# Splitting the first channel product of an MLP-mixer kernel into 49 block products on two levels instead of seven on one

**Chip and metric.** One core of one Trainium2 chip. The metric is the device time of one launch in microseconds (us); lower is better.

## What is computed

Attention without softmax, a root-mean-square norm, then an MLP mixer: first over tokens, then over channels. All in fp32.

```python
kv  = einsum('bhsd,bhse->bhde', k, v)            # B=8, H=8, S=576, D=64
out = einsum('bhsd,bhde->bhse', q, kv)
x   = out / sqrt(mean(out*out, -1) + 1e-6) * g_norm      # -> (B, S, 512)
u   = x + (relu(x.T @ w_tok1) @ w_tok2).T                # token mixing, 576 -> 256 -> 576
y   = u + relu(u @ w_ch1) @ w_ch2                        # channel mixing, 512 -> 1536 -> 512
```

The channel mixing is nine groups of 512 tokens, each one 512x512x1536 product (the "first" product), a relu, and one 512x1536x512 product (the "second").

## The kernel before

Both channel products are done with seven block products in place of eight (Strassen's scheme, in Winograd's form): the operands are cut in 2x2 blocks, sums of the blocks are formed (`mix_ch1`, `mix_ch2` for the weights once, `mix_u` for the tokens in each group), seven block products run on TensorE, and their results are combined. VectorE adds PSUM (where the kernel's matmuls put their sums) to what ScalarE copied out to SBUF (where its other tiles lie). Besides the four blocks of the relu the second product needs sums of them, `s1` to `s4`.

```python
def channel1(g, d):                         # three times a group, each for 512 of the 1536 columns
    ...
    def product(n, ps, start, stop):
        for w in range(W):                  # W = 2
            for c in range(2):
                nc.tensor.matmul(ps[:, w], lhsT=w_ch1[:, n - 1, c, ts(W * d + w, P)],
                                 rhs=uc[g][n - 1][:, c], ...)        # 256 tokens
    product(1, p1, True, False);  nc.scalar.copy(t1, p1)
    product(6, p6, True, True);   add(u2, p6, t1)
    product(7, p7, True, False);  add(u3, p7, u2)
    product(5, p5, True, False);  add(a22, p5, u3);  nc.scalar.activation(a22, a22, AF.Relu)
    product(2, p1, False, True);  nc.scalar.activation(a11, p1, AF.Relu)
    product(4, p7, False, True);  add(a12, p7, u2);  nc.scalar.activation(a12, a12, AF.Relu)
    product(3, p5, False, True);  add(s3, p5, u2)
    # max-and-add: relu of s3 and the sum in one instruction of VectorE, 512 columns
    nc.vector.scalar_tensor_tensor(out=s1, in0=s3, scalar=0.0, in1=a22, op0=max, op1=add)
    nc.vector.scalar_tensor_tensor(out=s3, in0=s3, scalar=0.0, in1=a11, op0=max, op1=subtract)
    nc.gpsimd.tensor_tensor(out=s2, in0=s1, in1=a11, op=subtract)
    nc.gpsimd.tensor_tensor(out=s4, in0=a12, in1=s2, op=subtract)
# (cut: channel2, with the same seven steps; attention; token mixing; decoding of the weights)
```

Of the kernel before, what the change touches and what calls it, by code (L numbers as in the profile page):

```python
# [9 lines left out]
F32 = mybir.dt.float32  # L10
U32 = mybir.dt.uint32
AF = mybir.ActivationFunctionType
# [5 lines left out]
def kernel(  # L18
# [29 lines left out]

    nc = tc.nc
    P = 128  # L50
# [11 lines left out]
    FH = DCH // 2  # L62
    NS = NF // 2
# [11 lines left out]
    stage = pool("stage", 2, "right")  # L75
    right = ExitStack()
    xp = pool("xp", 9, "right", right)
    hp_ = pool("hp", 2, "right", right)
    left = ExitStack()
# [9 lines left out]
    w_tok1 = consts.tile([P, JJ, DTOK], F32, name="w_tok1")  # L89
    w_tok2 = consts.tile([P, NTOK, S], F32, name="w_tok2")  # L90

    w_ch1 = consts.tile([P, 7, 2, FH], F32, name="w_ch1")
    w_ch2 = consts.tile([P, 7, NS, DH], F32, name="w_ch2")
# [5 lines left out]
    def do(f, *a):  # L99
        return lambda: f(*a)  # L100

# [72 lines left out]



    A1 = {(0, 0): 0, (0, 1): 1, (1, 1): 3, (1, 0): 6}
    B2 = {(0, 0): 0, (1, 0): 1, (1, 1): 2, (0, 1): 6}

    FQ = FH // 2  # L180

    def get_ch1(i, c, h):
        return block(FQ, lambda raw: [(raw, words(moe_w_ch1)[ts(c, P), ts(2 * i + h, FQ)])],
                     w_ch1[:, A1[i, c // 2], c % 2, ts(h, FQ)])

    def get_ch2(f):
        a, b = B2[f // NS, 0], B2[f // NS, 1]
        return block(DM, lambda raw: [(raw, words(moe_w_ch2)[ts(f, P)])],
                     w_ch2[:, a:b + 1:b - a, f % NS],
                     lambda raw: raw.rearrange("p (h n) w -> p h n w", h=2))  # L190

    def combine(o, a, b, op):
        nc.vector.tensor_tensor(out=o, in0=a, in1=b, op=op)  # L193

    def mix_ch1(c):
        w = [w_ch1[:, i, c] for i in range(7)]
        combine(w[4], w[6], w[3], ALU.add)
        combine(w[5], w[4], w[0], ALU.subtract)
        combine(w[6], w[0], w[6], ALU.subtract)
        combine(w[2], w[1], w[5], ALU.subtract)  # L200

    def mix_ch2(i):

        w = [w_ch2[:, n, 2 * i:2 * i + 2] for n in range(7)]
        combine(w[4], w[6], w[0], ALU.subtract)
        combine(w[5], w[2], w[4], ALU.subtract)
        combine(w[6], w[6], w[2], ALU.subtract)
        combine(w[3], w[1], w[5], ALU.subtract)
# [8 lines left out]
    def attention(pair):  # L217
# [13 lines left out]
        def norm(o_ps, c, n):  # L231
            o = o_ps.rearrange("p t (h d) -> p (t h) d", d=D)
            x = X[pair, c] = xp.tile([P, n, DM], F32, name="x", tag=f"x{n}", bufs=9 if n == 2 else 2)
            x3 = x.rearrange("p t (h d) -> p (t h) d", d=D)
            shape = [P, n * H, 1]
            nc.scalar.activation(x3, o, AF.Square)
            ms = work.tile(shape, F32, name="ms")
            nc.vector.tensor_reduce(ms, x3, axis=AX.X, op=ALU.add)  # L238
            nc.vector.tensor_scalar(out=ms, in0=ms, scalar1=1.0 / D, scalar2=EPS,
                                    op0=ALU.mult, op1=ALU.add)  # L240

            root = work.tile(shape, F32, name="root")
            nc.scalar.activation(root, ms, AF.Sqrt)
            inv = work.tile(shape, F32, name="inv")
            nc.vector.reciprocal(inv, root)
            nc.vector.scalar_tensor_tensor(out=ms, in0=ms, scalar=0.5, in1=inv,
                                           op0=ALU.mult, op1=ALU.mult)
            nc.vector.scalar_tensor_tensor(out=root, in0=root, scalar=0.5, in1=ms,
                                           op0=ALU.mult, op1=ALU.add)
            nc.vector.reciprocal(inv, root)  # L250
            nc.vector.tensor_mul(x3, o, inv.to_broadcast([P, n * H, D]))  # L251
            nc.gpsimd.tensor_mul(x3, x3, g_sb.to_broadcast([P, n * H, D]))  # L252
# [77 lines left out]
    def turn_u(g, i, psum):  # L330
        if i == 0:
            uT[g] = late["u"].tile([P, NC, J * P], F32, name="uT")
        pt = psum()
        for c in range(NC):
            nc.tensor.transpose(pt[:, c], xg[g][:, i, ts(c, P)], ident)  # L335
        nc.scalar.copy(uT[g][:, :, ts(i, P)], pt)  # L336

    def mix_u(g):
        b = {(i, j): uT[g][:, 2 * i:2 * i + 2, ts(j, 2 * P)] for i in range(2) for j in range(2)}
        t1, t2, t4 = (late["u"].tile([P, 2, 2 * P], F32, name=f"t{i}") for i in (1, 2, 4))  # L340
        sub = lambda o, x, y: nc.vector.tensor_tensor(out=o, in0=x, in1=y, op=ALU.subtract)
        sub(t1, b[0, 1], b[0, 0])
        sub(t2, b[1, 1], t1)
        sub(b[0, 1], b[1, 1], b[0, 1])
        sub(t4, b[1, 0], t2)
        uc[g] = [b[0, 0], b[1, 0], b[1, 1], t4, t1, t2, b[0, 1]]

    def prepare(g, psum):
        if g >= NG:
            return []  # L350
        return [do(turn_u, g, i, psum) for i in range(J)] + [do(mix_u, g)]
# [9 lines left out]
    def tmp(shape, name):  # L361
        return late["tmp"].tile(shape, F32, name=name)

    def channel1(g, d):

        W, N = 2, 2 * P
        shape = [P, W, N]
        a11, a12, a22, s1, s2, s3, s4 = (
            late["v"].tile(shape, F32, name=f"v{n}_{d}")
            for n in ("11", "12", "22", "s1", "s2", "s3", "s4"))  # L370
        V[g, d] = [a11, a12, s4, a22, s1, s2, s3]

        def product(n, ps, start, stop):
            for w in range(W):
                for c in range(2):
                    nc.tensor.matmul(ps[:, w], lhsT=w_ch1[:, n - 1, c, ts(W * d + w, P)],  # L376
                                     rhs=uc[g][n - 1][:, c], start=(start and w == 0 and c == 0),
                                     stop=stop, skip_group_check=True)

        add = lambda o, ps, x: nc.vector.tensor_tensor(out=o, in0=ps, in1=x, op=ALU.add)  # L380
        p1, p6, p7, p5 = (m_psum(shape, f"ps_v{n}") for n in (1, 6, 7, 5))
        t1, u2, u3 = tmp(shape, "t1"), tmp(shape, "u2"), tmp(shape, "u3")
        product(1, p1, True, False)
        nc.scalar.copy(t1, p1)
        product(6, p6, True, True)
        add(u2, p6, t1)
        product(7, p7, True, False)
        add(u3, p7, u2)
        product(5, p5, True, False)
        add(a22, p5, u3)  # L390
        nc.scalar.activation(a22, a22, AF.Relu)
        product(2, p1, False, True)
        nc.scalar.activation(a11, p1, AF.Relu)
        product(4, p7, False, True)
        add(a12, p7, u2)
        nc.scalar.activation(a12, a12, AF.Relu)
        product(3, p5, False, True)
        add(s3, p5, u2)

        nc.vector.scalar_tensor_tensor(out=s1, in0=s3, scalar=0.0, in1=a22,  # L400
                                       op0=ALU.max, op1=ALU.add)
        nc.vector.scalar_tensor_tensor(out=s3, in0=s3, scalar=0.0, in1=a11,
                                       op0=ALU.max, op1=ALU.subtract)
        nc.gpsimd.tensor_tensor(out=s2, in0=s1, in1=a11, op=ALU.subtract)  # L404
        nc.gpsimd.tensor_tensor(out=s4, in0=a12, in1=s2, op=ALU.subtract)

    def channel2(g):
# [4 lines left out]
        def product(n, ps, start, stop):  # L412
            for p in range(2):
                for s in range(NS):
                    nc.tensor.matmul(ps[:, p], lhsT=V[g, s // 2][n - 1][:, s % 2, ts(p, P)],  # L415
                                     rhs=w_ch2[:, n - 1, s], start=(start and p == 0 and s == 0),
# [5 lines left out]
        t1, u2, u3 = tmp(shape, "t1"), tmp(shape, "u2"), tmp(shape, "u3")  # L422
# [79 lines left out]
    ch1 = [get_ch1(i, c, h) for c in range(NC) for i in range(2) for h in range(2)]  # L502
    ch2 = [get_ch2(f) for i in range(3) for f in (2 * i, 2 * i + 1, NS + 2 * i, NS + 2 * i + 1)]
    mixes = [[do(mix_ch2, i)] for i in range(3)]
# [6 lines left out]
    weave(steps, staggered(ch1) + [do(mix_ch1, c) for c in range(2)])  # L511


    late = {}
    left.close()
    late["xg"] = pool("xg", 3)
    late["u"] = pool("u", 1)
    fetch_u(0)
    weights = [w for i in range(3) for w in staggered(ch2[4 * i:4 * i + 4]) + mixes[i]]
    cut = len(weights) // 2  # L520
    steps = run(last, token_mixing(3))
    extra = prepare(0, lambda: ps["o"].tile([P, NC, P], F32, name="ps_ut", tag="o"))
    weave(steps[:5], weights[:cut // 3])
    woven = []
    weave([do(woven.append, f) for f in steps[5:]], [do(woven.append, f) for f in extra])
    weave(woven, weights[cut // 3:cut])
# [3 lines left out]
    late["tmp"] = pool("tmp", 2)  # L530
    late["m"] = pool("m", 6, space=bass.MemoryType.PSUM)
    late["t"] = pool("t", 2, space=bass.MemoryType.PSUM)
    for g in range(NG):
        fetch_u(g + 1)
        weave([do(channel1, g, d) for d in range(NS // 2)], weights[cut:] if g == 0 else [])
        weave(channel2(g), prepare(g + 1, t_psum))
# [35 lines left out]
```

## Time and profile before

| | before |
|---|---|
| time, median of 4 runs beside the changed kernel | 937.73 us (937.48 to 938.46) |
| first matmul of the channel stage | 261.91 us |
| first matmul of one group to that of the next | 74.38 us once, then 74.28 us |
| mean granted TensorE clock (share of full speed) | 0.979 |

The busy times of the page, each with its share of the span and its number of instructions:

```profile
PE 883.5 (95%) x4128; PEld 722.8 (77%) x4128; DVE 388.9 (42%) x625; ACT 148.9 (16%) x260; POOL 227.0 (24%) x177
```

TensorE (PE) is at 95% (PEld is its own weight loads), all other engines are under half. In the channel stage the trace shows no wait of TensorE (from 262 to 935 us it is busy for 666.9 us of 673, at full clock), so only less work for TensorE can shorten it. The prediction shows the slices, the windows and the timeline behind that.

### The profile page before, as it was taken

The page shows a single profiled execution, that of the slowest core. Times are in us where ns is not written, and L with a number is a line of the kernel's source. Part 1 is how long each engine was busy: PE and PEld are TensorE (multiplying, and loading weights), DVE is VectorE, ACT ScalarE, POOL GpSimd, SP SyncE. Part 2 cuts the span into 40 slices and gives each one's busy share as a digit, 9 for nine tenths or more (in the row PEclk, how much of TensorE's full clock was granted, in tenths as well). Part 3 has the DMA queues.
Part 4 walks back from the last instruction along what each step waited for, and adds up shares of the span by engine and source line. Part 5 has one row for each costly group of instructions (what it writes and reads, how often), then busy time and mean ns, then how long its engine had stood idle before and what let it go on. Part 6 is the DMA issues. An engine that isn't in the chain of part 4 may idle for free.

```text
span 934.6 us, 10129 instructions
## 1 busy us (share of the span) xinstructions
PE 883.5 (95%) x4128; PEld 722.8 (77%) x4128; DVE 388.9 (42%) x625; ACT 148.9 (16%) x260; POOL 227.0 (24%) x177
## 2 busy tenths in 40 slices
PE   4698979968999999999999999999999999999997
PEld 3565555644478888888888888888888888888886
DVE  2858789899343133124123223213314303412411
ACT  2122132221111012011102102101101101100110
POOL 1535454554212102202202201211211220220220
PEclk9799989979999999999999999999999999999999
DMA  8777847634310020020011001001002001001001
GB/s 270 243 253 248 276 145 264 232 113 159 145 56 1 1 91 1 1 90 0 1 52 39 1 23 68 1 20 71 1 1 90 1 1 45 1 1 46 1 1 45
DMA packets 43566, 72.38 MB, mean 77 GB/s; under 512 B 2688, under 2 KB 21120, under 8 KB 43520
## 3 DMA queue, kind: packets, MB, share of 16 engines
q1 hardware_dynamic: 43376, 71.71, 23.0%
q8 instruction: 32, 0.52, 0.2%
q14 instruction: 14, 0.11, 0.0%
q10 hardware_dynamic: 144, 0.03, 0.0%
HBM read 52.85 MB, written 18.87 MB: 77 GB/s over the span
## 4 chain that ended last, share of the span: by engine, by line
PE 80%; DVE 13%; DMA 3%; issue 2%; POOL 2%; ACT 1%; SPq 0%; DVEq 0%; ACTq 0%
PE ps_v L376 35%; PE ps_w L415 35%; PE ps_h L284 3%; PE ps_u L302 2%; PE ps_kv L224 2%; DVE part L137 2%; PE ps_ut L335 2%; DVE x L251 2%; DVE ms L238 1%; DVE x L311 1%; DVE part L139 1%; DMA raw<-in_moe_w_tok_dram 1%; DVE w_ch L135 1%; PE ps_o L259 1%; DVE w_ch L193 1%
## 5 line engine op out<-in xcount | busy, mean ns | idle before, releaser
L376 PE MATMUL ps_v<-uT,w_ch 128*128 128x256 f32 x864 | 201.3, 379 | 0.0
L415 PE MATMUL ps_w<-w_ch,vs 128*128 128x256 f32 x864 | 192.1, 379 | 0.0
L376 PEld LDWEIGHTS ps_v<-uT,w_ch 128*128 128x128 f32 x864 | 164.4, 190 | 22.8 <-issue 0.8
L415 PEld LDWEIGHTS ps_w<-w_ch,vs 128*128 128x128 f32 x864 | 162.6, 190 | 20.8
L376 PE MATMUL ps_v<-t,w_ch 128*128 128x256 f32 x648 | 153.1, 379 | 0.0
L404 POOL TENSOR_TENSOR vs<-vs,v 128x512 f32<-128x512 f32 x27 | 47.9, 1774 | 418.9 <-DVE vs L400 410.0
L415 PE MATMUL ps_w<-w_ch,v 128*128 128x256 f32 x648 | 144.1, 379 | 0.0
L376 PEld LDWEIGHTS ps_v<-t,w_ch 128*128 128x128 f32 x648 | 123.3, 190 | 16.6
L415 PEld LDWEIGHTS ps_w<-w_ch,v 128*128 128x128 f32 x648 | 122.7, 190 | 16.1
L380 DVE TENSOR_TENSOR v<-ps_v,u 128x512 f32<-128x512 f32 x54 | 37.3, 691 | 102.1 <-PE ps_v L376 102.1
L224 PE MATMUL ps_kv<-v_in,k_in 128*128 128x128 f32 x320 | 47.6, 315 | 27.4 <-ACT kvp L228 18.0
L224 PEld LDWEIGHTS ps_kv<-v_in,k_in 128*128 128x128 f32 x320 | 45.3, 227 | 34.5 <-ACT kvp L228 19.7
L420 POOL TENSOR_TENSOR xg<-xg,u 128x512 f32<-128x512 f32 x27 | 33.8, 1264 | 135.3 <-DVE u L419 135.3
L419 DVE TENSOR_TENSOR xg<-ps_w,xg 128x512 f32<-128x512 f32 x27 | 18.7, 691 | 104.9 <-PE ps_w L415 104.9
L302 PE MATMUL ps_u<-h,w_tok 128*128 128x512 f32 x128 | 58.7, 604 | 0.0
L284 PE MATMUL ps_h<-x,w_tok 128*128 128x512 f32 x128 | 57.7, 596 | 0.6 <-POOL x L252 0.5
L252 POOL TENSOR_TENSOR x<-x,g_sb 128x1024 f32<-128x1024 f32 (+1 forms) x20 | 45.3, 2266 | 51.8 <-DVE x L251 38.0
L336 ACT COPY uT<-ps_ut 128x512 f32<-128x512 f32 x36 | 21.1, 585 | 214.8 <-PE ps_ut L335 214.8
L259 PEld LDWEIGHTS ps_o<-kvp,qT 128*128 128x128 f32 x256 | 33.9, 210 | 24.1 <-issue 13.9
L259 PE MATMUL ps_o<-kvp,qT 128*128 128x128 f32 x256 | 35.9, 298 | 17.4 <-DVE x L251 17.4
L419 DVE TENSOR_TENSOR u<-ps_w,u 128x512 f32<-128x512 f32 x18 | 12.4, 692 | 87.2 <-PE ps_w L415 87.2
L284 PEld LDWEIGHTS ps_h<-x,w_tok 128*128 128x128 f32 x128 | 23.3, 190 | 26.5 <-issue 23.4
(64 smaller groups left out, 665.1 us busy)
## 6 DMA issues: line engine op xcount, KB each, us to landing
qT<-in_q_dram SPq DMA_DIRECT2D x8, 1152.0 KB, 7.3
xg<-u_dram SPq DMA_DIRECT2D x9, 1024.0 KB, 5.7
k_in<-in_k_dram SPq DMA_DIRECT2D x16, 512.0 KB, 3.9
v_in<-in_v_dram SPq DMA_DIRECT2D x16, 512.0 KB, 5.7
u_dram<-x SPq DMA_DIRECT2D x16, 512.0 KB, 3.0
out_dram<-xg SPq DMA_DIRECT2D x16, 512.0 KB, 2.8
raw<-in_moe_w_ch_dram SPq DMA_DIRECT2D x16, 384.0 KB, 5.0
raw<-in_moe_w_ch_dram SPq DMA_DIRECT2D x12, 512.0 KB, 4.2
```

The lines of the kernel that those rows point to most:

```text
L224: nc.tensor.matmul(acc[:, i], lhsT=kk[:, j, ts(i, P)], rhs=vv[:, j, ts(i, P)], start=(j == 0), stop=(j == JJ - 1))
L252: nc.gpsimd.tensor_mul(x3, x3, g_sb.to_broadcast([P, n * H, D]))
L259: nc.tensor.matmul(o[:, t, ts(hp, P)], lhsT=qT[2 * pair + side][:, hp, ts(2 * (c % 2) + t, P)], rhs=kvp[side][:, hp], start=True, stop=True)
L284: nc.tensor.matmul(acc[side, t], lhsT=w_tok1[:, j, ts(t, P)], rhs=x_of(pair, side * J + j), start=(j == 0), stop=False)
L302: nc.tensor.matmul(acc_u, lhsT=w_tok2[:, t, ts(i % J, P)], rhs=h1[i // J][:, t], start=(t == 0), stop=(t == NTOK - 1))
L336: nc.scalar.copy(uT[g][:, :, ts(i, P)], pt)
L376: nc.tensor.matmul(ps[:, w], lhsT=w_ch1[:, n - 1, c, ts(W * d + w, P)], rhs=uc[g][n - 1][:, c], start=(start and w == 0 and c == 0), stop= ...
L380: add = lambda o, ps, x: nc.vector.tensor_tensor(out=o, in0=ps, in1=x, op=ALU.add)
L404: nc.gpsimd.tensor_tensor(out=s2, in0=s1, in1=a11, op=ALU.subtract)
L415: nc.tensor.matmul(ps[:, p], lhsT=V[g, s // 2][n - 1][:, s % 2, ts(p, P)], rhs=w_ch2[:, n - 1, s], start=(start and p == 0 and s == 0), st ...
L419: add = lambda o, ps, y: nc.vector.tensor_tensor(out=o, in0=ps, in1=y, op=ALU.add)
L420: padd = lambda o, a, b: nc.gpsimd.tensor_tensor(out=o, in0=a, in1=b, op=ALU.add)
```

## The change

*Intent.* Apply the same scheme once more inside each of the seven block products of the first product: 49 block products of 128 tokens. In columns streamed, 49 x 3 x 128 takes the place of 7 x 12 x 256, an eighth less. The price is more sums on VectorE and GpSimd. The seven outer products run in the order 1, 6, 7, 5, 2, 3, 4; I number them k = 0 to 6 by their place. The sums of the weights for both levels move to the end of the first pass and into the first group.

```diff
-    def channel1(g, d):  ... seven products of 256 tokens, for each third of the columns
+    def channel1(g):
+        padd = lambda o, a, b: nc.gpsimd.tensor_tensor(out=o[:, 1:], in0=a[:, 1:], in1=b[:, 1:], op=ALU.add)
+        def after5():                       # behind outer product 5, k = 3
+            padd(s3, a22, s1)
+            padd(a22, a22, a12)
+            relu(a22)                       # ScalarE
+        def after3():                       # behind outer product 3, k = 5
+            padd(s3, s3, s4)
+            nc.vector.scalar_tensor_tensor(out=s1, in0=s3, scalar=0.0, in1=a22, op0=ALU.max, op1=ALU.add)
+            nc.vector.scalar_tensor_tensor(out=s3, in0=s3, scalar=0.0, in1=a11, op0=ALU.max, op1=ALU.subtract)
+            nc.gpsimd.tensor_tensor(out=s2, in0=s1, in1=a11, op=ALU.subtract)
+        ...                                 # after6, after7, after2, after4: sums of 1152 on GpSimd
+        def outer(o):                       # seven inner products in seven steps
+            def product(n, ps, start, stop):
+                for w in range(W):          # W = 3
+                    nc.tensor.matmul(ps[:, w], lhsT=a_of(o, n)[:, ts(w, P)],
+                                     rhs=uT[g][:, SB[o], SB[n]], ...)        # 128 tokens
+            ...                             # copy t1 (ScalarE), adds of 384 columns from PSUM (VectorE)
+    def mix_u(g, level):                    # token sums, now on both levels
+        if level == 1:
+            return [step() for step in t_sums(lambda n: uT[g][:, SB[n], :4])]
+        return [step() for step in t_sums(lambda n: uT[g][:, :, SB[n]])]
+    def mix_ch2():                          # weight sums of the second product, now on GpSimd
+        ...
+    # end of the first pass: VectorE's weight sums woven into the last token mixing
+    late["d2"] = pool("d2", 1, "right").tile([P, 3, NS, DH], F32, name="d2")
+    mixes = mix_ch2()                       # issued during the first group
 # (cut: the layout of the weights, the pools, fetch buffers of token rows 3 -> 2)
```

## The prediction

> **What bounds the kernel now.** I read the digits of the forty slices first, then busy time by stretch, the groups of instructions, and the timeline of one channel group.
>
> ```profile
> PE   4698979968999999999999999999999999999997
> DVE  2858789899343133124123223213314303412411
> PEclk9799989979999999999999999999999999999999
> ```
>
> ```profile
> 0.00:262.00 262.00, 216.60 (x977) 134.86 (x977) 198.16 (x347) 59.01 (x111) 111.12 (x96) 0.93 0.65 212
> 262.00:935.00 673.00, 666.91 (x3152) 587.90 (x3152) 190.76 (x279) 89.91 (x149) 115.85 (x81) 1.00 0.07 25
> ```
>
> There are two stages (columns: length, then busy time of PE, PEld, DVE, ACT, POOL, clock, DMA share, GB/s). Up to 262 us (attention, token mixing, weight decoding) the VectorE sets the pace; the chain of waits there is mostly DVE. From 262 us on, nine channel groups run and TensorE never pauses. A group is 36.3 us of first product, 36.3 us of second product and four sets of transposes of 0.43 us: 74.3 us (the first product of one group starts at 336.29, of the next at 410.57).
>
> ```profile
> 338.02 1.89 PE L376 MATMUL ps_v<-t,w_ch 128*128 128x256 f32 x8
> 339.74 1.89 PE L376 MATMUL ps_v<-uT,w_ch 128*128 128x256 f32 x8
> ```
>
> ```profile
> 101.06 2.31 PEld L224 LDWEIGHTS ps_kv<-v_in,k_in 128*128 128x128 f32 x20 [0.81 <-issue]
> 103.29 0.30 PEld L284 LDWEIGHTS ps_h<-x,w_tok 128*128 128x128 f32 x2
> ```
>
> Starts, not durations, give the rate, since matmuls overlap. Every fp32 matmul leaves two records. With 256 tokens a record costs (339.74-338.02)/8 = 215 ns; with 128 tokens and a new weight each time, (103.29-101.06)/20 = 111.5 ns.
>
> [...]
>
> ```profile
> 156.19 2.17 PE L259 MATMUL ps_o<-kvp,qT 128*128 128x128 f32 x14 [2.27 <-DVE x L251]
> 157.50:160.80 3.30, 3.30 (x13) 1.77 (x13) 3.30 (x6) 1.59 (x2) 1.68 (x2) 0.50 0.32 123
> ```
>
> After an idle 2.27 us the clock is 0.50 for some 3.4 us; idles of 2.97 and 3.34 us did the same, one of 2.06 us did not. [...]
>
> ```profile
> 190.15 2.87 POOL L141 TENSOR_TENSOR w_ch<-w_ch,part 128x512 f32<-128x512 f32 x2 [2.83 <-DVE part L139]
> 191.83 3.35 DVE L193 TENSOR_TENSOR w_ch<-w_ch 128x512 f32<-128x512 f32 x3 [1.16 <-POOL w_ch L141]
> 350.17 0.69 DVE L402 SCALAR_TENSOR_TENSOR vs<-vs,v 128x512 f32<-128x512 f32 x1
> 350.21 1.77 POOL L404 TENSOR_TENSOR vs<-vs,v 128x512 f32<-128x512 f32 x1 [28.11 <-DVE vs L400]
> ```
>
> The first of the three L193 took 1.73 us instead of 0.65, because GpSimd was in the middle of L141; at 350.2 VectorE came first and GpSimd took 1.77 us instead of 1.26. L405, which overlaps adds from PSUM, stays at 1.27 us: those do not collide. [...] the trace has 691 ns at 512[...].
>
> **The change, part by part.** (a) *Fewer columns on TensorE.* Per group 84 matmuls of 256 tokens become 147 of 128: 168 x 215.9 ns = 36.28 us becomes 294 x 111.5 ns = 32.8 us. Minus 3.5 us a group, minus 31 us in all, if nothing waits. The second product is as before.
>
> (b) *More combining.* Per group VectorE gets 42 adds of 384 from PSUM (23.4 us), two max-and-add of 1536 (3.5 us), eight sums of token blocks (7.1 us) and the second product's six adds (4.1 us): 38 us of 70, no bound in the sum. GpSimd gets seven adds of 1152 and two subtractions of 1536. From 1.266 us at 512 and 2.342 us at 1024 (L252, lowest) I get 2.105 ns an element plus 0.19 us: 2.61 and 3.42 us, together 25 us. ScalarE gets relus of 1536, 1.48 us (0.63 at 512, 0.83 ns an element). So the averages are harmless; the order within a group decides.
>
> (c) *Walking through one group* with the compiled order of each engine, outer products k = 0 to 6 of 4.68 us each (seven inner products of 0.67 us), 0 = first matmul. Latencies are from the trace: PE to DVE or ACT 0.27 us, DVE to PE 0.14, DVE to POOL 0.15, others 0.1. For k = 0 to 4 VectorE follows with 3.3 to 4.0 us per 4.68, no wait. First stall: the last add of k = 3 (one add more, seven) ends at 19.98; GpSimd adds 20.13-22.74 and 22.82-25.43; the relu of that result runs 25.5-27.0. ScalarE's order puts this relu ahead of the PSUM copy of k = 5, ready at 24.3. The copy ends at 27.5, so the fifth inner product of k = 5 waits 1.6 us and the sixth 0.6 us: k = 5 ends at 30.3 instead of 28.1. Second stall: its last add ends at 31.1, GpSimd adds until 33.9, and only then does VectorE's first max-and-add run, 34.0-35.8, ahead of the third add of k = 6 in VectorE's order. TensorE does a quarter of the second product's first block product and waits 1.6 us until 36.5. Third: GpSimd starts its 3.42 us subtraction at 35.9; the second max-and-add, two SBUF inputs, comes at 36.4, is locked out until 39.3 and ends at 41.0; the add behind it ends at 41.6. TensorE, after another quarter, waits 38.45 to 41.74, 3.3 us. Sum of waits 7.1 us. The first product and the first block of the second end at 45.0 us, against 36.28+5.18 = 41.5 before: **plus 3.5 us a group**, the gain of 3.5 eaten twice.
>
> (d) *Clock.* The third wait leaves a hole of some 3.1 us with another of 1.4 us just before it. By the holes above, an aligned window that idles for 2 us or more halves the clock for the next; with a random phase I put that at three groups in four, some 1.6 us each: plus 1.2 us a group.
>
> (e) *First pass.* The weight sums leave the middle: 8 of 768 and 9 of the 12 of 512 ran there before the last normalization, 16.5 us of VectorE at their recorded means. Behind it the new sums lie mostly in idle VectorE time, but the compiled order puts four sums of 1536 (7.0 us) and three of 384 (1.7 us) between the last normalization's steps, and the last decoded block before them (2.2 us). Net 5.6 us of work less; since some of these sums stand in gaps of waiting for ScalarE, I count minus 5 us. Against it the first group must await all eight token sums, 7.1 us instead of 2.8 us: plus 2.5 us. Net minus 2.5 us.
>
> (f) *Transfers*: the fetch buffers go from three to two, but a fetch has over 30 us before its transposes and takes 5.7 us: nothing.
>
> Sum: 937.8 - 2.5 + 9 x (3.5 + 1.2) = 977.6; I say **975 us**, since part of the second stall may be shorter.
>
> **Rivals.** *The waits vanish*: the author's queues hide them and TensorE stays bound; then 937.8 - 31 - 2.5 = 904 us. For it: VectorE and GpSimd are far from full, and TensorE never waited before. Against it: three orders of the compiled program, each in-order, and durations from the trace. *The waits come, the lock does not*: GpSimd yields to the second max-and-add as at 350.2. Then the third wait is some 1 us and the clock stays: 9 x 1.2 - 2.5 gives about 946 us. Against it: GpSimd has half a microsecond of head start. *The clock stays full*: 9 x 3.5 - 2.5, about 967 us. *Weights bind*: if loads of 128 columns could not keep 111.5 ns with three of them per moving block, TensorE itself would lose the gain; the runs of twenty at L224 speak against it.
>
> **Range and chances.** The lock and the clock together move the result from 946 to 978 and a wait of half a microsecond more or less per group by 4.5 us; the first pass may err by 7 us. 8 in 10: 946 to 992 us. Over 2% faster (under 919) needs nearly all three waits to be absent: 0.05. Within 2% (919 to 956.5): the lock absent or the waits half as long, 0.17. Slower: 0.78.
>
> **What would show it.** In the new profile, records of the first product should start 111 to 112 ns apart inside a product (step a). The time from one group's first matmul to the next should be 78 to 79 us, not 74.3. TensorE should show three waits per group, in k = 5 behind ScalarE's copy and in k = 6 twice behind VectorE; one of the two 1536 max-and-add should last 4 to 4.6 us and the other 1.76 us; the clock should be at half for 3.4 us after many of the holes; the channel stage should start at about 259 us. I am wrong if TensorE is unbroken (then 904), if the second max-and-add lasts 1.76 us (then 946), or if waits appear in k = 0 to 4, which I have as free.

## The result, and the profile after

The changed kernel takes **984.0 us** (median of 4 runs, 982.0 to 984.27), 1.0487 times the time before (95% interval 1.0469 to 1.0506): slower. A ratio is the mean time of one kernel's runs over that of the other's of the same rounds, so not quite the ratio of the medians quoted.

| | before | after |
|---|---|---|
| first matmul of the channel stage | 261.91 | 261.34 |
| first group | 74.38 | 88.86 |
| each later group | 74.28 | 78.46 to 78.50 |
| mean clock | 0.979 | 0.962 |

The nine groups are the whole loss: eight later ones of +4.2 us and a first one of +14.5 us, less 0.6 us at the start, make 47.5 us, and the spans differ by 47.6.

The page after: the busy times, and the slices of TensorE and of its clock. They answer to the lines of before shown above and in the prediction.

```profile
PE 880.3 (90%) x5262; PEld 741.7 (76%) x5262; DVE 575.1 (59%) x880; ACT 155.4 (16%) x251; POOL 385.9 (39%) x212
...
PE   3798979798797998999899899899899899899987
...
PEclk9899989899989999999999999999999999999999
```

TensorE's row of nines now has an eight in most groups, and no engine beside it is anywhere near full. That points to an order of events rather than to throughput; the experiments test it. What TensorE waits for from 225 us to the end (columns: the wait and its releaser; us in total, number, longest):

```profile
PE ps_v L451 <- DVE vs L401: 26.6, 9, 3.0
PE ps_v L451 <- DVE u L401: 11.6, 18, 1.0
PE ps_v L451 <- DVE uT L191: 6.9, 1, 6.9
PE ps_v L451 <- ACT t L459: 5.9, 9, 0.8
```

The first and the last come once a group, the second twice; the third is the first group's alone. One steady group (its first matmul is at 350.20), at the end of k = 6. TensorE's timeline of the changed kernel (start, length, line, output and inputs, number of records, and in brackets the idle time before it and its releaser):

```profile
385.59 0.94 PE L451 MATMUL ps_v<-uT,w_ch 128*128 128x128 f32 x6 [0.97 <-DVE u L401]
386.37 1.46 PE L507 MATMUL ps_w<-w_ch,v 128*128 128x256 f32 x6
390.78 0.94 PE L451 MATMUL ps_v<-uT,w 128*128 128x128 f32 x6 [2.95 <-DVE vs L401]
391.55 4.44 PE L507 MATMUL ps_w<-w_ch,v 128*128 128x256 f32 x12
```

The same moment on VectorE, on GpSimd (POOL) and, somewhat earlier, on ScalarE (ACT):

```profile
383.31 1.76 DVE L426 SCALAR_TENSOR_TENSOR vs<-vs,v 128x1536 f32<-128x1536 f32 x1 [1.33 <-POOL vs L402]
384.99 0.55 DVE L401 TENSOR_TENSOR u<-ps_v,u 128x384 f32<-128x384 f32 x1
385.46 4.80 DVE L428 SCALAR_TENSOR_TENSOR vs<-vs,v 128x1536 f32<-128x1536 f32 x1
390.18 0.54 DVE L401 TENSOR_TENSOR vs<-ps_v,u 128x384 f32<-128x384 f32 x1
```

```profile
385.21 3.43 POOL L430 TENSOR_TENSOR vs<-vs,v 128x1536 f32<-128x1536 f32 x1 [1.94 <-DVE vs L426]
```

```profile
375.21 1.48 ACT L404 ACTIVATE v<-v 128x1536 f32<-128x1536 f32 x1 [4.91 <-POOL v L402]
376.60 0.46 ACT L459 COPY t<-ps_v 128x384 f32<-128x384 f32 x1
```

L426 and L428 are the two max-and-adds, of one shape: one takes 1.76 us, the other 4.80. GpSimd's subtraction began 0.25 us before the second and ended at 388.64; the max-and-add ended 1.62 us after that. Behind it, in VectorE's queue, stands the add of 390.18, which frees the accumulator that TensorE waits for until 390.78. Then twelve records of the second product (L507) take 4.28 us (391.55 to the next start, 395.83) instead of 12 x 215.5 ns = 2.59: the clock is at half. On ScalarE the copy that TensorE's inner product needs starts only when a relu of 1536 has left, and TensorE waits 0.62 and 0.32 us there.

The first group has a wait of its own. GpSimd's weight sums, VectorE's token sums and TensorE of the changed kernel:

```profile
251.67 3.58 POOL L191 TENSOR_TENSOR d<-w_ch 128x768 f32<-128x768 f32 x2 [14.32 <-DMA u_dram<-x]
...
263.63 4.86 POOL L191 TENSOR_TENSOR d<-w_ch,d 128x768 f32<-128x768 f32 x2
```

```profile
264.75 2.09 DVE L191 TENSOR_TENSOR uT<-uT 128x896 f32<-128x896 f32 x1
```

```profile
269.50 1.65 PE L451 MATMUL ps_v<-uT,w 128*128 128x128 f32 x6 [6.90 <-DVE uT L191]
```

A token sum of 896 columns takes 1.09 us in later groups; here it takes 2.1, and the same sums of GpSimd go from 1.79 us each to 2.43. They hinder each other, though they share no tile (d and w_ch here, uT there), just where the channel stage waits for the last token sum. This is what the prediction and the experiments call the lock: instructions of VectorE with two inputs in SBUF and of GpSimd that overlap and then take longer. In the trace of before GpSimd's L404 took 1.77 us beside L402 (L405, of the same shape, 1.26 beside an add from PSUM), and VectorE's L193 1.73 us beside L141 (the shortest of its shape 0.63); here L428 takes 4.80 us beside L430 instead of 1.76. The clock is at half from 265.48 to 275.71.

### The profile page after: what moved, and what is told of

The parts are those of the page before. It is cut to its first block, busy times and chain, and to the rows that moved or that the text cites. A ratio compares the mean times of both kernels' runs of the same rounds, so it can differ in the third digit from the quotient of the medians.

```text
span 982.2 us, 12730 instructions
## 1 busy us (share of the span) xinstructions
PE 880.3 (90%) x5262; PEld 741.7 (76%) x5262; DVE 575.1 (59%) x880; ACT 155.4 (16%) x251; POOL 385.9 (39%) x212
## 4 chain that ended last, share of the span: by engine, by line
PE 52%; issue 7%; POOL 6%; DVE 3%; ACT 0%; DVEq 0%; POOLq 0%
PE ps_w L507 32%; PE ps_v L451 18%; POOL vs L402 4%; POOL v L402 2%; DVE u L401 1%; PE ps_ut L362 1%; DVE vs L401 1%; ACT t L459 0%; DVE xg L511 0%; DVE vs L428 0%; DVE vs L426 0%; ACT v L404 0%; DVEq L401 0%; POOLq L402 0%
## 5 line engine op out<-in xcount | busy, mean ns | idle before, releaser
L451 PE MATMUL ps_v<-uT,w 128*128 128x128 f32 x1782 | 224.6, 278 | 42.3 <-DVE vs L401 26.6
L451 PEld LDWEIGHTS ps_v<-uT,w 128*128 128x128 f32 x1782 | 210.9, 193 | 49.6 <-DVE vs L401 30.2
L451 PE MATMUL ps_v<-uT,w_ch 128*128 128x128 f32 x864 | 118.1, 278 | 8.7 <-DVE u L401 8.7
L451 PEld LDWEIGHTS ps_v<-uT,w_ch 128*128 128x128 f32 x864 | 107.9, 194 | 13.5 <-DVE u L401 12.3
L507 PE MATMUL ps_w<-w_ch,v 128*128 128x256 f32 x432 | 113.9, 420 | 0.0
L402 POOL TENSOR_TENSOR vs<-vs,v 128x1152 f32<-128x1152 f32 x9 | 23.7, 2629 | 205.6 <-DVE vs L401 205.6
L507 PEld LDWEIGHTS ps_w<-w_ch,v 128*128 128x128 f32 x432 | 89.7, 214 | 13.8
L507 PE MATMUL ps_w<-d,vs 128*128 128x256 f32 x432 | 96.2, 379 | 0.0
L507 PE MATMUL ps_w<-w_ch,vs 128*128 128x256 f32 x432 | 96.2, 379 | 0.0
L402 POOL TENSOR_TENSOR v<-v,vs 128x1152 f32<-128x1152 f32 x27 | 70.9, 2628 | 53.4 <-DVE vs L401 34.2
L507 PEld LDWEIGHTS ps_w<-w_ch,vs 128*128 128x128 f32 x432 | 81.5, 190 | 10.7
L507 PEld LDWEIGHTS ps_w<-d,vs 128*128 128x128 f32 x432 | 80.9, 190 | 10.4
L191 DVE TENSOR_TENSOR uT<-uT 128x512 f32<-128x512 f32 (+1 forms) x72 | 74.6, 1067 | 4.1 <-ACT uT L364 3.3
L404 ACT ACTIVATE v<-v 128x1536 f32<-128x1536 f32 x27 | 40.1, 1484 | 164.8 <-POOL v L402 164.8
L401 DVE TENSOR_TENSOR vs<-ps_v,u 128x384 f32<-128x384 f32 x108 | 59.9, 554 | 9.2 <-PE ps_v L451 0.6
```

The costliest lines, as they stand in the source:

```text
L191: engine.tensor_tensor(out=o, in0=a, in1=b, op=op)
L401: add = lambda o, ps, x: nc.vector.tensor_tensor(out=o, in0=ps, in1=x, op=ALU.add)
L402: padd = lambda o, a, b: nc.gpsimd.tensor_tensor(out=o[:, 1:], in0=a[:, 1:], in1=b[:, 1:], op=ALU.add)
L404: relu = lambda o: nc.scalar.activation(o, o, AF.Relu)
L451: nc.tensor.matmul(ps[:, w], lhsT=a_of(o, n)[:, ts(w, P)], rhs=uT[g][:, SB[o], SB[n]], start=(start and w == 0), stop=stop, skip_group_che ...
L507: nc.tensor.matmul(ps[:, p], lhsT=V[g][n - 1][:, 2 * (s // W) + p, s % W], rhs=w2_of(n)[:, s], start=(start and p == 0 and s == 0), stop=s ...
```

## Experiments

The theory to test: (1) the second max-and-add is locked out by GpSimd; (2) the relu ahead of the copy on ScalarE makes the first waits; (3) the holes, not a load, halve the clock; (4) GpSimd's weight sums spoil the first group; (5) VectorE's weight sums at the end of the first pass hold up the last normalization. The rival to all is that there is simply too much work beside TensorE. Every edit below is an edit of the changed kernel, and every result is correct.

### e1: GpSimd's subtraction after the second max-and-add

```diff
-            nc.gpsimd.tensor_tensor(out=s2, in0=s1, in1=a11, op=ALU.subtract)
+            nc.gpsimd.tensor_tensor(out=s2, in0=s3, in1=a22, op=ALU.add)     # same value, later input
```

> One edit: GpSimd forms the same matrix s2 from the outcome of the second max-and-add (s3 + a22) instead of from the first (s1 - a11), so it cannot start before the second max-and-add has ended. My theory (the second max-and-add is locked out of the memory by GpSimd's 3.42 us subtraction): the second max-and-add takes 1.76 us instead of 4.80, TensorE's third wait falls from 2.95 us to about 0.2, the half clock that followed it goes (1.7 us), each group takes about 74.0 us instead of 78.5, the kernel about 943 us (938 to 960). Rival (the second max-and-add is slow of itself, by its operands or its place): it stays at 4.8 us and the time at 984.

Measured: 940.15 us (939.16 to 941.41), 1.0022 of before; a later group takes 73.73 us. VectorE and GpSimd of this run:

```profile
378.61 1.75 DVE L428 SCALAR_TENSOR_TENSOR vs<-vs,v 128x1536 f32<-128x1536 f32 x1
```

```profile
380.53 3.44 POOL L430 TENSOR_TENSOR vs<-vs,v 128x1536 f32<-128x1536 f32 x1 [4.09 <-DVE vs L428]
```

The second max-and-add has the same operands and the same place (behind the same add), and takes 1.75 us. The third wait and the half clock behind it are gone: the twelve records of the second product take 2.60 us (381.65 to 384.25) instead of 4.28, and the mean clock is 0.979, as before the change, instead of 0.962. One instruction's start time was worth 44 us: the lock is the largest single cause. GpSimd is busy for 384.5 us here and for 385.9 in the changed kernel, so it is not the amount of its work. (In the changed kernel the two also read `a11` at the same time. That this alone kept one of them back is unlikely, since the first group's sums collide without a shared tile.)

### e2: the relu behind the copy on ScalarE

```diff
         def after5():
             padd(a22, a22, a12)
-            relu(a22)
         def after3():
+            with tc.issue_after(seen["t1", 3]):      # order only: queue it behind the copy of t1
+                relu(a22)
```

> One edit: relu(a22) on ScalarE is queued behind the copy of t1 of the fifth outer product (o = 3), not ahead of it. My theory: the first pair of waits of a group (0.62 + 0.32 us behind ScalarE's copy) goes, and the rest of the chain in the sixth product only moves: the group takes 77.0 to 78 us instead of 78.5, the kernel 970 to 980. Rival (the two later waits are measured from GpSimd's sum, which does not move, so the 0.9 us come back as longer waits there): the group stays at 78.5 us and the time at 984, with the first pair of waits gone and the others longer by as much.

Measured: 966.22 us, in two pairs: 962.88 and 963.67 at a mean clock of 0.971, 968.77 and 969.37 at 0.962. Neither side had that number. TensorE's waits of this run from 340 to 900 us:

```profile
PE ps_v L452 <- DVE vs L401: 20.7, 7, 3.0
PE ps_v L452 <- DVE u L401: 6.8, 7, 1.0
```

The two waits behind ScalarE's copy are gone and the others are unchanged (0.97 and 2.95), so they do not come back, and the rival falls. But four later groups of the profiled run take 75.30 us and three take 76.7 to 77.0, with one and the same hole of 2.95 us in each. The difference is the clock. The windows of e2 (start:end, length, busy time of PE, PEld, DVE, ACT, POOL, clock, DMA share, GB/s) around that hole, first in a 75.30 us group:

```profile
382.90:386.32 3.42, 1.60 (x9) 1.10 (x8) 3.42 (x1) 0.00 (x0) 2.42 (x1) 1.00 0.00 0
386.32:389.73 3.41, 2.28 (x13) 2.11 (x14) 2.57 (x5) 0.00 (x0) 0.67 (x1) 1.00 0.00 0
```

then in a 76.99 us group:

```profile
686.69:690.09 3.40, 1.43 (x10) 1.35 (x11) 3.30 (x5) 0.00 (x0) 0.00 (x0) 1.00 0.00 0
690.11:693.50 3.39, 3.39 (x10) 2.67 (x9) 0.09 (x1) 0.58 (x1) 2.61 (x1) 0.50 0.00 0
```

The stretches lie on one grid of 3.413 us, which I took from the clock changes of the record: in the trace of before the clock goes to half at 24.34, 96.02, 130.15, 157.46, 191.59, 222.31 and 932.28 us, which is 21, 31, 39, 49, 58 and 266 stretches after the first. Here, where the grid cut the hole so that no stretch idled more than 1.82 us (1.82 and 1.13), the clock stayed full; where one idled 1.97 us, the next ran at half. In the traces of before and of the changed kernel, from 20 us on, every stretch that idled 2.14 us or more was followed by half clock; of the stretches at full clock, those that idled 1.98 us or less were followed by full clock. So the border is blurred: 1.98 us (changed kernel, 214.27 to 217.68) was followed by full clock, the 1.97 us of e2 by half. (A stretch at half clock was followed by another after less: 0.61 us in the changed kernel, 268.89 to 272.30.) I read the idle time from modelled ends, so no closer than 0.1 us. In the changed kernel a group of 78.48 us is almost exactly 23 stretches (78.51), so the hole falls on nearly the same place of the grid each time, and every group is hit, always 78.5 us apart (391.77, 470.27, 548.78 us and so on). In e2 75.30 us is 22 stretches and 0.2 us, so the hole slides until it is hit. The half clock costs 76.99 - 75.30 = 1.7 us a group.

### e3: e1 and e2 together

> The edits of e1 (GpSimd's subtraction after the second max-and-add) and e2 (relu behind the copy) together, to see whether the two causes add. My theory (the ScalarE wait, 0.63 + 0.32 us a group, is independent of the lock): a group takes 72.7 to 72.9 us, 0.95 less than the 73.74 of e1, and with nine groups the kernel 930 to 933 us; the one wait left is 0.97 us behind the first max-and-add. Rival (the 3.2 us a group that e2 won alone were another path that e1 already took away, or the wait returns behind the first max-and-add): the group stays at 73.7 and the time at 940.

Measured: 927.56 us (926.4 to 928.46), 0.9889 of before; a later group takes 72.24 us. The causes add, and by more than I expected: 1.5 us a group beyond e1, where the removed waits are 0.95. A hole costs more than the wait shown for it. The version without a hole that the profile shows (e5, 71.04 us) gives the size: e3 has one wait of 0.97 us and is 1.20 longer; e1 has three, 1.92 us in sum, and is 2.70 longer. That is 0.23 to 0.26 us for each hole. The trace shows two parts. The wait is counted from the modelled end of the last record, but in an unbroken stream the next record starts 0.16 us before that end (381.15 to 381.82 in the changed kernel: starts 0.67 us apart, 0.83 us long). And six records behind a hole take 0.77 us to the next start (390.78 to 391.55), not 0.67.

### e4: GpSimd's weight sums after the first outer product

```diff
-    late["d2"] = pool("d2", 1, "right").tile([P, 3, NS, DH], F32, name="d2")
-    mixes = mix_ch2()
+    d2p = pool("d2", 1, "right")
+    hold = d2p.tile([P, 3, NS, DH], F32, name="hold", tag="d2")    # used as t1 of k = 0, group 0
     ...
+            if g == 0 and n == 1:                                  # from the second outer product on
+                late["d2"] = d2p.tile([P, 3, NS, DH], F32, name="d2", tag="d2")
+                mixes = mix_ch2()
```

> One edit: the memory of the second product's three extra weight blocks is held back for one copy, so that GpSimd's weight sums (8 of 768 columns) start after the first outer product of the first group, not before it, beside VectorE's token sums. My theory: the token sums take 0.7 and 1.1 us again instead of 2.1 to 2.3, TensorE's wait of 6.9 us in front of the first group's products goes, and so does most of its half clock; the first group takes 80 to 82 us instead of 88.9, the others stay at 78.5, the kernel 975 to 978 us. Rival (the first group waits for its token rows' transfer or for the weight blocks, not for the lock): it stays at 88.9 and 984.

Measured: 977.25 us (974.62 to 979.98). VectorE and TensorE of this run:

```profile
262.59 3.09 DVE L191 TENSOR_TENSOR uT<-uT 128x896 f32<-128x896 f32 x3
```

```profile
263.73 0.94 PE L451 MATMUL ps_v<-uT,w 128*128 128x128 f32 x6 [0.64 <-DVE uT L191]
...
292.98 0.58 PE L451 MATMUL ps_v<-uT,w 128*128 128x128 f32 x1 [3.13 <-ACT t L460]
```

Three token sums in 3.09 us: the lock is gone and the wait of 6.90 us has become 0.64. The first group takes 83.38 us, a little above the 80 to 82 expected, because GpSimd's delayed sums push the relu of k = 3 back and the wait behind ScalarE grows to 3.13 us, once. The later groups are as before, except where the hole falls well on the grid (one takes 76.77).

### e6: more work for VectorE

```diff
-                add(to[:, 2], at["p7"], at["u2"])
+                for _ in range(2 if o in (1, 6, 7, 2) else 1):
+                    add(to[:, 2], at["p7"], at["u2"])
```

> A load test: in four of the seven outer products of each group, an add of VectorE that can be repeated without changing the result is done twice, about 2.2 us of VectorE more in each group. My theory (VectorE's mere load does not bind, the order behind the sums does): the time stays at 984 within 4 us. Rival (VectorE at 59% is the bound of the group's middle): each group takes about 2 us longer, the kernel 1000 us or more.

Measured: 984.16 us (983.92 to 986.13), as the changed kernel. The busy times of its page:

```profile
PE 880.2 (90%) x5262; PEld 742.2 (76%) x5262; DVE 592.3 (60%) x916; ACT 155.3 (16%) x251; POOL 386.0 (39%) x212
```

VectorE did 17 us more and the time stayed the same. In these four outer products (k = 0, 1, 2 and 4) the mere load of VectorE is free; the rival of "too much work" falls for VectorE there, and e1 and e5 answer it for the rest: GpSimd has the same work in e1, and VectorE has more in e5 (577.9 us), where the waits are gone.

### e5: the long sums behind the last add, on VectorE

```diff
-            (both max-and-adds and GpSimd's s2 behind k = 5; GpSimd's padd(a12, a12, s4) behind k = 6)
+            with tc.issue_after(seen["to1", 4]):     # behind the last add of k = 6
+                max-and-add s1;  s2 = s1 - a11 (VectorE);  last = max-and-add s3
+            with tc.issue_after(last):
+                nc.vector.tensor_tensor(out=a12[:, 1:], in0=a12[:, 1:], in1=s4[:, 1:], op=ALU.add)
+            (and the relu behind the copy, as in e2)
```

> The relu behind the copy as in e2, and both max-and-adds, the subtraction s2 and the last sum of a12 on VectorE, queued behind the last add of the sixth outer product: nothing of the sums stands ahead of an add that frees an accumulator, and GpSimd takes no lock beside them. My theory (order behind the long sums is the whole cost of the steady group): no wait of TensorE in the group, no half clock, a group of 70.9 to 71.6 us (294 records of 111.5 ns, 168 of 215.5 ns, 1.9 us of transposes), the kernel 915 to 924 us, 13 us or more below e1 and e2 together would be too much: e3 minus 9 x 1.0 to 1.6. Rival (the 2.5 us of GpSimd work moved to VectorE, and the later sums, only move the wait into the second product, whose second block needs s2): a wait of over 1 us at the first records of the second product, group 72.5 to 74, the kernel 932 to 945.

Measured: 916.53 us (915.16 to 917.31), 0.9771 of before (0.9757 to 0.9784); later groups of 71.03 to 71.05 us. TensorE and VectorE of this run, behind k = 6:

```profile
373.89 5.34 PE L509 MATMUL ps_w<-w_ch,v 128*128 128x256 f32 x24
```

```profile
373.45 1.20 DVE L401 TENSOR_TENSOR vs<-ps_v,u 128x384 f32<-128x384 f32 x2
374.57 1.75 DVE L429 SCALAR_TENSOR_TENSOR vs<-vs,v 128x1536 f32<-128x1536 f32 x1
```

It is 11.0 us below e3, 1.2 for each group, within what was expected. All 24 records of the second product's first block stand together: no wait shown, no half clock (they start 5.18 us before what follows, 24 x 215.8 ns). The long sums have 5.2 us of TensorE's work to hide behind, and they fit. The change's intent is sound: 74.28 - 71.04 = 3.24 us a group is what the smaller product is worth. This kernel differs from the changed one only in order and in the engine of two sums.

### e8: VectorE's weight sums behind the last normalization

```diff
-            nc.vector.tensor_mul(x3, o, inv.to_broadcast([P, n * H, D]))
+            seen["norm"] = nc.vector.tensor_mul(x3, o, inv.to_broadcast([P, n * H, D])).ins
     ...
+    def behind_norm(step):
+        with tc.issue_after(seen["norm"]):
+            step()
-           for f in mix_ch1() + [step for o in ORDER[:2] for step in mix_ch1_of(o)]])
+           for f in [do(behind_norm, step) for step in mix_ch1() + [... the same ...]]])
```

> One edit in the changed kernel: VectorE's weight sums for the first product (four of 1536 columns, eight of 384) are queued behind the last normalization's last step, not between its steps. My theory (the sums held up the last normalization, by 4.7 us of the 5 gained): the last normalized rows come 4 to 6 us earlier, the 2.96 us wait of TensorE before the last token mixing goes, and the kernel takes 978 to 981 us, unless the sums then hold up the transposes in front of the channel stage. Rival (the end of the first pass is bound elsewhere, by the token sums and GpSimd's weight sums at 255 to 269 us): the time stays at 984 within 2 us, the 2.96 us come back as a longer wait in front of the first group's products.

Measured: 982.38 us (980.29 to 983.5); nothing that counts beside 984.0. Here the rival was right. The channel stage's first matmul comes at 258.98 instead of 261.34, but (GpSimd and TensorE of this run):

```profile
252.14 3.89 POOL L191 TENSOR_TENSOR d<-w_ch 128x768 f32<-128x768 f32 x2 [18.54 <-DMA u_dram<-x]
```

```profile
270.60 1.65 PE L451 MATMUL ps_v<-uT,w 128*128 128x128 f32 x6 [10.36 <-DVE uT L191]
```

GpSimd's sums start 0.5 us later than in the changed kernel and keep the token sums back 1.1 us longer (TensorE goes on at 270.60, not 269.50), so the wait in front of the second block of products grows from 6.90 to 10.36 us, more than the 2.4 us won.

One profile of the first pass must not be read too closely. In the eight profiled runs without this edit (the changed kernel, e1 to e6, e10) the channel stage starts between 259.65 and 263.19 us; in the three with it (e8, e9, e11) between 256.62 and 258.98. So the earlier start is the edit's. TensorE's wait before the last token mixing is 1.58 us here and 2.96 in the changed kernel, but 1.3 to 1.4 in e1, e4, e5 and e6, whose first pass is without this edit too: that this wait fell because of the edit is not shown.

### e9, e10, e11: all together, and which of the first-pass edits matter

> All the edits together: the sums of the sixth outer product behind its last add and on VectorE, the relu behind the copy, GpSimd's weight sums after the first outer product, VectorE's weight sums behind the last normalization. If the causes found are all there are: steady groups of 70.9 to 71.6 us, a first group of 73 to 77, a channel start at 255 to 261 us, 904 to 916 us, faster than the kernel before by 2 to 3.5%. If the moves at the end of the first pass do not add: 915 to 922.

> The best version (905.8 us) without the edit of e8: the order of the sums inside the group as in e5, and GpSimd's weight sums after the first outer product as in e4. My theory (the order of VectorE's weight sums, worth nothing by itself because the stage waited for the token sums anyway, is worth its 4 to 5 us once that wait is gone): 909 to 911.5 us, the channel stage starts at 260 to 262 us instead of 256.7. Rival (the edit of e8 is worth nothing in any setting): 905 to 907.

> The best version (905.8 us) without the edit of e4: the order inside the group as in e5, and VectorE's weight sums behind the last normalization as in e8, but GpSimd's weight sums beside the token sums. My theory (GpSimd's sums hold the lock from 252 to 270 us whatever comes before, so the stage's second product starts at 268 to 270.5 us all the same): 914.5 to 917 us, as e5 (916.5), with TensorE's wait in front of the first group's second block of products at about 10 us. Rival (the two edits add): 911 to 913.

All four have the order of e5 inside the group (e5 and e9 ran on one chip, e10 and e11 on another; the kernel before took 938.03 and 938.26 us beside them):

| | VectorE's weight sums as in the change | behind the normalization (e8) |
|---|---|---|
| GpSimd's weight sums as in the change | e5: 916.53 | e11: 915.80 |
| after the first outer product (e4) | e10: 911.37 | **e9: 905.84** |

e8's edit is worth 0.7 us alone (no more than noise: the runs of e5 and e11 overlap) and 5.5 us beside e4's; e4's is worth 5.2 alone and 10.0 beside e8's. TensorE's timeline says why, in e11 and then in e10:

```profile
268.23 1.65 PE L453 MATMUL ps_v<-uT,w 128*128 128x128 f32 x6 [10.36 <-DVE uT L191]
```

```profile
239.25 5.40 PE L311 MATMUL ps_h<-x,w_tok 128*128 128x512 f32 x8 [2.96 <-POOL x L279]
```

The first line is the later hole, which e4's edit removes. The second lies in the first pass, where e8's edit gains its time (how much of it in this wait is not shown, see e8). They stand one behind the other. Filling the earlier one alone only lets TensorE arrive sooner at the later one. (In e10's profiled run the channel stage started at 263.19 us, outside the 260 to 262 expected; the time was as expected.)

**e9** is the best version: 905.84 us (905.46 to 907.31, five runs), 0.9661 of before (0.9648 to 0.9674), faster. TensorE's waits from 225 to 900 us:

```profile
PE ps_v L453 <- DVE uT L191: 1.5, 1, 1.5
PE ps_v L453 <- ACT t L462: 1.1, 1, 1.1
PE ps_v L453 <- DVE u L401: 0.3, 1, 0.3
```

The waits left are one each, in the first group (74.69 us; the others 71.04). Of the 30.8 us between its span (903.8) and that of before (934.6), the earlier start of the channel stage (256.66) gives 5.3, the seven groups after the first 7 x 3.24 = 22.7, and the last one with its end 3.2; the first group, 74.69 for 74.38, takes back 0.3.

## Why the prediction was right, and where it was off

The direction held, and so did the mechanism inside the group: 975 was predicted, 984 measured, inside the range. The first pass went wrong, and that the total is still so near is in part luck: the loss inside the group was over-estimated by 4.5 us in all, the first pass under-estimated by 12.3. Step by step:

- **(a) TensorE: minus 3.5 us a group.** Right: records of the first product start 111 to 112 ns apart, and the group without holes is 3.24 us shorter (e5, e9). Loading a new weight for every 128 tokens did not bind; that rival is out.
- **(b) The averages are harmless.** Right: e6, e1 and e5. The times that I took for VectorE's sums at 384, 896 and 1536 columns were my estimate; measured in the changed kernel are 0.55 to 0.56, 1.09 and 1.76 us.
- **(c) Three waits, 7.1 us.** All three came at the places named, and in the later groups nowhere in k = 0 to 4. (In the first group the wait of 6.90 us lies in k = 0, which I had as free; see (e).) Sizes, with 0.22 us added for each hole (what closes 78.47 - 71.04 = 7.43 us over four waits of 4.86 and the half clock's 1.69): the copy's two 1.4 us (predicted 2.2), the first max-and-add 1.2 (1.6), the lock 3.2 (3.3); 5.7 us in all. The durations from the trace held to a few hundredths (GpSimd 2.63 and 3.43 us for the 2.61 and 3.42 worked out), and the second max-and-add took 4.80 us, a little more than the 4 to 4.6 given. What I over-estimated is chiefly the wait behind ScalarE: the relu left 26.5 us after the group's first matmul (350.20 to 376.69), not 27.0, and the copy was done at 26.9, not 27.5. That the lock was the main part is shown by e1, that the relu's place was the first by e2; that the two are independent by e3.
- **(d) The clock: 1.2 us a group, three groups in four.** Under-estimated: 1.7 us in every group. I took the phase to be random; a group of nearly 23 grid stretches repeats it. A threshold of 2 us of idle in an aligned window was close (1.97 us was followed by half clock in e2, 1.98 by full clock in the changed kernel). The errors of (a), (c) and (d) partly cancel: together plus 4.2 us a group where I had plus 4.7. The three half clocks that the prediction lists, behind idles of 2.27, 2.97 and 3.34 us, last 3.41 us each in the trace of before. How long a hole is does not tell by itself: in the changed kernel one of 2.25 us (up to 217.96), cut by the grid to 1.98 and 0.27, and one of 2.61 us (up to 38.46), cut to 0.93 and 1.68, were followed by full clock.
- **(e) The first pass: minus 2.5 us. This step failed.** The channel stage started 0.6 us earlier, but the first group took 10.4 us more than a later one: about plus 9.8 in place of minus 2.5. The start lay above the 259 us given in all eight profiled runs without e8's edit (259.65 to 263.19): the minus 5 us counted for it did not come. The plus 2.5 for the token sums does not follow from the prediction's own figures either: 7.1 less 2.8 is 4.3. I had the token sums at durations without GpSimd beside them and did not look at what GpSimd would do beside them, though I used the same lock in (c). Its weight sums waited for a transfer, 14.3 us, because their memory was used before by rows still being written out, and so fell on the token sums. e4 takes that away; e8 to e11 show that some 5 us can be gained in the first pass, but only when VectorE's weight sums stand behind the last normalization, where the prediction did not have them, and this second hole is gone.
- **(f) Transfers.** Right for the fetches, no wait for them; wrong in that a transfer decided when GpSimd's sums began.

In the sum: 977.6, less 0.5 x 9 for (a), (c) and (d), plus 12.3 for (e), is 985.4. The figure of 975, lower than my own sum, rested on a shorter second stall, which came true (1.2 us for 1.6) and was outweighed by (e).

What is not settled: why the first group of e9 keeps 3.7 us over the later ones; its three waits of 2.9 us in sum, with some 0.25 us for each hole, would account for it, but I did not try to remove them.

## What to carry to other kernels

When TensorE's work is cut, look at each in-order queue beside it: does a long instruction stand ahead of one that frees an accumulator, and does a GpSimd instruction with SBUF inputs start just before a VectorE instruction with two SBUF inputs that TensorE will wait for (here 4.80 us instead of 1.76)? Here that, and not the amount of work, turned 3.2 us a group won into 4.2 us lost. Where a hole stays, look at the idle time in each stretch of the clock's grid, and at whether a loop's period is near a whole number of stretches: the same hole of 2.95 us cost 1.7 us more where one stretch idled 1.97 us, and nothing more where the grid split it 1.82 to 1.13 (e2); a period of 78.48 us against 23 x 3.413 repeated that loss in every group of the changed kernel. After removing one hole look for the next one behind it before judging the edit: two edits worth 0.7 and 5.2 us alone were worth 10.7 together.
